# Ranks computed beside the counts, independent stores, and record scatters moved later, in a sigmoid-attention and top-1 MoE kernel

## The chip, the cores and the metric

The kernel runs on one core of one Trainium2 chip. The metric is the device time of one execution in microseconds (us). Three runs of the kernel before took 776.0, 776.97 and 777.6 us; their median, 776.97 us, is the time before. Engines are named as the profile names them: PE (TensorE matmul), PEld (its weight load), DVE (VectorE), ACT (ScalarE), POOL (GpSimd) and SP (SyncE, which here only issues DMAs).

## The reference

```python
# q, k, v: (8 batches, 12 heads, 448 tokens, 64); w_gate (768, 8); w1 (8, 768, 1024); w2 (8, 1024, 768)
scores = scale * np.matmul(q, k.transpose(0, 1, 3, 2)) - np.log(S)
attn = 1.0 / (1.0 + np.exp(-scores))
x = matmul(attn, v).transpose(0, 2, 1, 3).reshape(3584, 768)
logits = x @ w_gate
expert_idx = np.argmax(logits, axis=1)
gate_w = softmax(logits)[expert_idx]            # one weight per token
for e in range(8):                              # every token goes through its own expert only
    mask = expert_idx == e
    out[mask] = gate_w[mask, None] * (np.maximum(x[mask] @ w1[e], 0.0) @ w2[e])
```

## The kernel before, in words

**Two streams on PE.** Attention is cut into 168 steps. A step is one chunk of 64 keys for two pairs of heads: `scores(s)` (L616) and `weighted(s)` (L632), each with matmuls on 64x64 quarters of the array, which show as 8 records in each of the two lines. Seven steps finish two pairs of heads, 21 steps (`PB`) a batch. Steps 0 to 69 run attention alone, in the order written in `attention()`; from step 70 (`START`) each step also yields 14 matmuls of the dense part (`MIX`), and the seven attention chunks of two pairs come in one burst, once in seven steps. The dense part, `moe(b, wts)` (L240 and L263), takes seven batches of tokens through the expert that most of their tokens chose, with 448-column matmuls in three float32r terms. Its w1 loop runs over 8 columns j of 18 matmuls, and its weights come as raw tiles over SP, are split into a high part by ACT (L159) and a low part by POOL or DVE (L160), three w1 columns ahead. Whatever token did not choose that expert goes through two items of 256 rows at the end (`large`), found through a list of records.

**The gate of a batch** is a chain of small stages that `PLACES` puts at fixed steps: `gate_a` (logits, psg, L291), `gate_b` (transposed logits pl, L300, and the one-hot choice `oh`), `gate_c` (a matmul of `ones` by `oh`, L335, gives the counts; their maximum gives the expert), `gate_c2` (the mask `ce` and `lm = oh * ce`, the tokens that need a record), `gate_c3` (the gate weights), `gate_d` (two control matmuls of `upper` and of `ones` by `lm`, L388 and L389, then the ranks from PSUM, L392 to L403, giving the slot indices `si`), `gate_d2` s0 to s3 (POOL's indirect scatter of the records, L424, after an iota on POOL and a copy of the gates by DVE, L416), and `gate_g`, `gate_e` (the gate rows). The psg, pl, pc and pr tiles are taken by `small_ps` out of the four PSUM buffers `sc` of the scores. `upper` and `ones` are full 128-wide operands, so these matmuls use the whole array and stand between the quarter-array ones of attention or the dense ones.

**Queues.** All instructions stand in the order written (`manual_schedule`). SP issues weights, q, k, v, the token stores `x_tok<-xt` (L499, four DMAs for every three pairs of heads, 64 in all), the slot loads `raw<-x_tok` (L465) and the output stores (L218, 84). POOL issues some of the k and v loads before step 70, the records, and the low parts. `apart` declares that a store need not wait for earlier ones in a list: one list for each of the 12 column blocks (`stored`), and `taken[i]` one for each quarter of the token rows.

**Records before.** `PUTS` puts batch 0's four scatters at steps 34 to 40 and batch 1's at steps 56 to 62 (their places 13, 15, 17, 19 made even), while attention runs alone; those of batches 2 to 7 stand in the dense part. The tiles `si` and `rec` have two buffers each.

Of the kernel before, what the change touches and what calls it, by code (L numbers as in the profile page):

```python
# [18 lines left out]
P = 128  # L19
# [5 lines left out]
def tile_sigmoid_attention_top1_moe(  # L25
# [182 lines left out]
                self.split += 1  # L208

    stores = []  # L210
    stored = {}
    out_b = out.rearrange("(b j r) f -> b r j f", b=B, r=32)

    def store():
        if stores:
            n, d, i, ob = stores.pop(0)
            cols = slice(d * DW + i * DW // 4, d * DW + (i + 1) * DW // 4)
            put = nc.sync.dma_start(  # L218
                out_b[bass.ds(maps[n], 1)][:, :, :, cols].rearrange("o r j f -> (o r) j f"),
                ob.rearrange("p j s t -> p j (s t)")[32 * i : 32 * (i + 1)],  # L220
            )
            apart(put, stored.setdefault((d, i), []))

    def moe(b, wts):

# [101 lines left out]
    def gate_c(b, oh, z):  # L327
        def tl(nm, shape, dt=F32):
            return small.tile(shape, dt, tag=nm, name=f"{nm}_{b}")

        s1, s2 = tl("s1", [GP, NCH, E]), tl("s2", [GP, NCH, E])
        nc.scalar.activation(s1, z, AF.Sigmoid)
        nc.scalar.activation(s2, z, AF.Sigmoid, scale=-1.0)
        pc = small_ps(b, "pc")
        nc.tensor.matmul(pc[:, : NCH * E], ones[:GP], oh.rearrange("p c e -> p (c e)"), start=True, stop=True)  # L335
        cnt = tl("cnt", [P, E])
        nc.vector.tensor_reduce(cnt, pc[:, : NCH * E].rearrange("p (c e) -> p e c", e=E), axis=AX.X, op=ALU.add)
        cm = tl("cm", [P, 1])
        nc.vector.tensor_reduce(cm, cnt, axis=AX.X, op=ALU.max)
        ce = tl("ce", [P, E])  # L340
        nc.vector.scalar_tensor_tensor(ce, cnt, cm, rev, op0=ALU.is_equal, op1=ALU.mult)
        cr, was, now = top[:, b : b + 1], free[:, b : b + 1], free[:, b + 1 : b + 2]
        nc.vector.tensor_reduce(cr, ce, axis=AX.X, op=ALU.max)
        ri = tl("ri", [P, 2], I32)
        if b > 0:
            rf = tl("rf", [P, 2])
            old = top[:, b - 1 : b]
            nc.vector.tensor_sub(rf[:, 0:1], old, cr)
            nc.vector.scalar_tensor_tensor(rf[:, 0:1], rf[:, 0:1], was, cr, op0=ALU.mult, op1=ALU.add)
            nc.vector.tensor_scalar(ri[:, 0:1], rf[:, 0:1], -1.0, float(E), op0=ALU.mult, op1=ALU.add)  # L350
            nc.vector.tensor_scalar(ri[:, 1:2], was, -1.0, float(b), op0=ALU.mult, op1=ALU.add)
        return s1, s2, ri, ce, cm

    def gate_c2(b, oh, s1, s2, ri, ce, cm):
        def tl(nm, shape, dt=F32):
            return small.tile(shape, dt, tag=nm, name=f"{nm}_{b}")

        cr, was, now = top[:, b : b + 1], free[:, b : b + 1], free[:, b + 1 : b + 2]
        nc.vector.tensor_scalar(ce, ce, cr, None, op0=ALU.is_equal)
        keep = tl("keep", [P, 1])  # L360
        if b < B - 1:
            nc.vector.scalar_tensor_tensor(keep, cm, float(2 * P), was, op0=ALU.is_le, op1=ALU.mult)
        else:
            nc.vector.tensor_copy(keep, was)
        nc.vector.tensor_sub(now, was, keep)
        nc.vector.tensor_scalar(keep, keep, -1.0, None, op0=ALU.add)
        nc.vector.tensor_scalar(ce, ce, keep, 1.0, op0=ALU.mult, op1=ALU.add)
        lm = tl("lm", [GP, NCH, E], BF16)
        nc.vector.tensor_tensor(lm, oh, ce[:GP].unsqueeze(1).broadcast_to([GP, NCH, E]), op=ALU.mult)
        return lm  # L370

    def gate_c3(b, s1, s2):
        nc.vector.reciprocal(s2, s2)
# [3 lines left out]
        nc.vector.tensor_scalar(sm, sm, 1e-9, None, op0=ALU.add)  # L377
        nc.vector.reciprocal(gates[:GP, b], sm)

    def gate_d(b, lm):  # L380

        def tl(nm, shape, dt=F32):
            return small.tile(shape, dt, tag=nm, name=f"{nm}_{b}")

        pr = small_ps(b, "pr")
        lmf = lm.rearrange("p c e -> p (c e)")
        nce = NCH * E
        nc.tensor.matmul(pr[:, :nce], upper[:GP], lmf, start=True, stop=True)  # L388
        nc.tensor.matmul(pr[:, nce : 2 * nce], ones[:GP], lmf, start=True, stop=True)  # L389
        pre = tl("pre", [P, NCH, E])  # L390
        tot = pr[:, nce : 2 * nce].rearrange("p (c e) -> p c e", e=E)
        nc.vector.tensor_copy(pre[:, 0], base)  # L392
        for c in range(1, NCH):
            nc.vector.tensor_add(pre[:, c], pre[:, c - 1], tot[:, c - 1])
        nc.vector.tensor_add(base, pre[:, NCH - 1], tot[:, NCH - 1])
        rk = tl("rk", [GP, NCH, E])
        nc.vector.tensor_add(rk, pre[:GP], pr[:GP, :nce].rearrange("p (c e) -> p c e", e=E))
        nc.vector.tensor_add(rk, rk, region[:GP])
        nc.vector.tensor_mul(rk, rk, lm)
        sl = tl("sl", [GP, NCH])  # L400
        nc.vector.tensor_reduce(sl, rk, axis=AX.X, op=ALU.add)
        si = small.tile([GP, NCH], U32, tag="si", bufs=2, name=f"si_{b}")
        nc.vector.tensor_scalar(si, sl, BIG, None, op0=ALU.add)  # L403
        return si
# [47 lines left out]
    xts = {}  # L452
    wholes = {}
    raws = {}
    taken = [[] for _ in range(4)]
    x_tok_b = x_tok.rearrange("(b j r) (i f) -> b i r j f", b=B, r=32, i=4)

    def load_slot(n, ri):
# [4 lines left out]
        for i in range(4):  # L463
# [1 line left out]
                raws[n][32 * i : 32 * (i + 1)].rearrange("r j t s -> r j (t s)"),  # L465
                x_tok_b[bass.ds(maps[n], 1), i].rearrange("o r j f -> (o r) j f"),
            )
            taken[i].append(got)

    low_parts = []  # L470

# [16 lines left out]
    def tokens(g, pv):  # L488
# [5 lines left out]
            xts[b] = xtpool.tile([P, NB, KH, 32], F32, tag="xt", bufs=2, name=f"xt_{b}_{n}")  # L494
        nc.vector.transpose(xts[b][:, :, t, :], pv[:, :S].rearrange("p (j s) -> p j s", s=32))  # L495
        if t == KH - 1:
            rows = x_tok[b * S : (b + 1) * S].rearrange("(j r) (i f) -> i r j f", r=32, i=4)
            for i in range(4):
                put = nc.sync.dma_start(  # L499
                    rows[i][:, :, n * KH * 32 : (n + 1) * KH * 32],  # L500
                    xts[b][32 * i : 32 * (i + 1)].rearrange("r j t s -> r j (t s)"),
                )
                for got in taken[i]:
                    tc.declare_no_dep(put.ins, got.ins, reason="the slots read earlier batches' tokens")

    def small_ps(b, name):

        return ps_sc.tile([P, 512], F32, tag="sc", name=f"{name}_{b}")
# [164 lines left out]
    def attention():  # L673
# [33 lines left out]
        def stage(what, b):  # L707
# [9 lines left out]
            elif what == "l" and b > 0:  # L717
                load_slot(b - 1, g["c"][2])
            elif what == "d":
                si_of[b] = gate_d(b, g["lm"])  # L720
            elif what[0] == "s":
                gate_d2(b, si_of[b], int(what[1]))
            elif what == "g" and b > 0:
# [3 lines left out]

        LATE = {8: "b", 10: "c", 11: ("l", "c2"), 12: "c3", 15: "d", 16: "g", 26: "e"}
        FOUR = ("s0", "s1", "s2", "s3")
        PUTS = 2 * (dict(zip((13, 15, 17, 19), FOUR)),) + 4 * (dict(zip((27, 28, 29, 30), FOUR)),)  # L730
        PUTS += (dict(zip((25, 26, 27, 28), FOUR)), {9: "s0", 10: "s1"})
        LAST = {3: "b", 5: "c", 6: ("l", "c2"), 7: "c3", 8: "d", 9: "g"}
        EARLY = {5: "b", 7: ("c", "c2"), 9: ("l", "c3"), 11: "d", 13: "g", 32: "e"}
# [26 lines left out]
        for s in range(N_ST + 11):  # L760
# [14 lines left out]
            elif s == START:  # L775
                weigh_to(a)
                score_to(a + 2)
                copy_tokens()
            yield s, MIX[0]
            if s >= START:  # L780
                b, r = divmod(s - 3 * PB, PB)
                b += 1
# [11 lines left out]
            if s in SPLITS:  # L794
                split_tokens(0, SPLITS.index(s), nc.vector.tensor_copy)
            yield s, MIX[1]
        order.close()

    wts = Weights([(lambda b=b: regs.get(b)) for b in range(B + 1)], NS)
# [382 lines left out]
```

## Time and profile before

| what | value |
|---|---|
| runs | 776.0, 776.97, 777.6 us (median 776.97) |
| the profiled execution's own time | 776.84 us |
| its span in the trace | 775.0 us |
| PE busy | 768.4 us (99%) |
| DVE, ACT, POOL busy | 373.9, 384.1, 349.6 us (48%, 50%, 45%) |
| granted TensorE clock | 1.00 (2.4 GHz) in nearly every stretch |
| DMA | 125.67 MB, mean 162 GB/s |

The span runs from the first to the last instruction. A matmul's busy time overlaps that of the next, so the distance from one start to the next is the measure of what an instruction costs PE, and the timeline shows these starts.

### The profile page before, as it was taken

How to read it: one execution, taken by the hardware profiler on the slowest of the kernel's cores; microseconds unless marked ns; L12 is line 12 of the kernel's file. 1: busy time of each engine (PE TensorE's matmuls, PEld its weight loads, DVE VectorE, ACT ScalarE, POOL GpSimd, SP SyncE). 2: the span in 40 equal slices, each digit the busy share in tenths (PEclk: the TensorE clock that was granted, in tenths of full speed). 3: DMA queues.
4: the chain of work that ended last, by engine and by line, in shares of the span. 5: the costliest groups of instructions: out<-in, count | busy, mean ns of one | idle time of the engine just before them, and what ended most of it. 6: DMA issues, size and time to landing. Idle time of an engine off the chain costs nothing. (4 is left out here: it accounts for less than half of the span.)

```text
span 775.0 us, 15532 instructions
## 1 busy us (share of the span) xinstructions
PE 768.4 (99%) x5586; PEld 593.3 (77%) x5586; DVE 373.9 (48%) x806; ACT 384.1 (50%) x688; POOL 349.6 (45%) x330
## 2 busy tenths in 40 slices
PE   9999999999999999999999999999999999999997
PEld 6555557687696786867868769677698999999996
DVE  2354584465264652537426384254736493244543
ACT  5877776645536455264443653545523342444451
POOL 8648554242352342531615316054265764664351
PEclk9999999999999999999999999999999999999999
DMA  9777798976758846587585876766167554655770
GB/s 207 169 160 157 171 251 197 210 171 154 169 129 173 201 107 166 139 190 168 116 194 84 193 169 144 183 168 166 38 171 170 157 146 118 202 143 155 220 223 38
DMA packets 311633, 125.67 MB, mean 162 GB/s; under 512 B 210062, under 2 KB 307006, under 8 KB 311552
## 3 DMA queue, kind: packets, MB, share of 16 engines
q1 hardware_dynamic: 305504, 112.42, 61.9%
q0 software_dynamic: 5760, 11.76, 5.4%
q8 instruction: 45, 0.74, 0.4%
q10 hardware_dynamic: 288, 0.46, 0.2%
q14 instruction: 36, 0.29, 0.1%
HBM read 102.49 MB, written 22.49 MB: 161 GB/s over the span
## 5 line engine op out<-in xcount | busy, mean ns | idle before, releaser
L602 ACT ACTIVATE at<-sc,bias_s 128x448 f32<-128x448 f32 x336 | 192.3, 633 | 107.4 <-PE sc L616 106.5
L160 POOL TENSOR_TENSOR w1l<-wst,w1h 128x768 fp32r<-128x768 f32 x72 | 132.7, 1853 | 173.9 <-ACT w1h L159 172.2
L160 POOL TENSOR_TENSOR w2l<-wst,w2h 128x512 fp32r<-128x512 f32 x84 | 107.0, 1298 | 138.7 <-ACT w2h L159 121.0
L616 PE MATMUL sc<-qt,kt 64*64 64x448 f32 x1344 | 167.3, 545 | 0.0
L632 PE MATMUL av<-at,vn 64*64 64x448 f32 x1344 | 165.0, 536 | 0.0
L240 PE MATMUL ps<-xh,w1h 128*128 128x448 f32 x336 | 124.4, 370 | 0.2 <-DVE nw L439 0.2
L240 PE MATMUL ps<-xh,w1l 128*128 128x448 f32 x336 | 123.4, 367 | 0.0
L240 PE MATMUL ps<-xl,w1h 128*128 128x448 f32 x336 | 123.3, 367 | 0.0
L263 PE MATMUL ps<-hh,w2l 128*128 128x448 f32 x336 | 123.3, 367 | 0.0
L263 PE MATMUL ps<-hl,w2h 128*128 128x448 f32 x336 | 123.2, 367 | 0.0
L263 PE MATMUL ps<-hh,w2h 128*128 128x448 f32 x336 | 122.7, 365 | 0.0
L616 PEld LDWEIGHTS sc<-qt,kt 64*64 64x64 f32 x1344 | 78.2, 189 | 56.9 <-issue 44.4
L632 PEld LDWEIGHTS av<-at,vn 64*64 64x64 f32 x1344 | 59.4, 133 | 64.3 <-issue 53.5
L159 ACT CAST w2h<-wst 128x512 fp32r<-128x512 f32 x108 | 64.7, 620 | 75.7 <-PE ps L263 64.5
L247 ACT ACTIVATE hh<-ps 128x448 fp32r<-128x448 f32 x56 | 30.6, 546 | 139.6 <-PE ps L240 137.0
L276 DVE TENSOR_TENSOR ps<-ps,gt 128x448 f32<-128x448 f32 x42 | 40.7, 969 | 85.4 <-PE ps L263 85.3
L495 DVE STREAM_TRANSPOSE xt<-av 128x448 f32<-128x448 f32 x46 | 27.3, 629 | 101.5 <-PE av L632 100.4
L248 DVE SCALAR_TENSOR_TENSOR hl<-ps,hh 128x448 fp32r<-128x448 f32 x56 | 34.4, 614 | 78.3 <-ACT hh L247 76.8
L240 PEld LDWEIGHTS ps<-xh,w1h 128*128 128x128 f32 x336 | 63.1, 188 | 9.9 <-issue 4.4
L263 PEld LDWEIGHTS ps<-hh,w2l 128*128 128x128 f32 x336 | 65.2, 194 | 6.6 <-issue 3.5
L263 PEld LDWEIGHTS ps<-hl,w2h 128*128 128x128 f32 x336 | 65.2, 194 | 6.2 <-issue 3.2
L263 PEld LDWEIGHTS ps<-hh,w2h 128*128 128x128 f32 x336 | 65.2, 194 | 3.4 <-DVE nw L439 0.2
(158 smaller groups left out, 918.9 us busy)
## 6 DMA issues: line engine op xcount, KB each, us to landing
wst<-in_moe_w_dram SPq DMA_DIRECT2D x72, 384.0 KB, 3.3
wst<-in_moe_w_dram SPq DMA_DIRECT2D x54, 512.0 KB, 5.1
x_tok<-xt SPq DMA_DIRECT2D x64, 168.0 KB, 2.8
qn<-in_q_dram SPq DMA_DIRECT2D x184, 56.0 KB, 3.1
raw<-x_tok SPq DMA_DIRECT2D x28, 336.0 KB, 6.2
out_dram<-ob SPq DMA_DIRECT2D x84, 112.0 KB, 2.4
kn<-in_k_dram SPq DMA_DIRECT2D x104, 56.0 KB, 3.3
kn<-in_k_dram POOLq DMA_DIRECT2D x80, 56.0 KB, 4.0
```

Of the source, the lines that this page charges most:

```text
L159: nc.scalar.copy(hi, st)
L160: eng.tensor_tensor(lo, st, hi.bitcast(F32), op=ALU.subtract)
L240: nc.tensor.matmul(ps[:, :S], a[:, ws], b_, start=(t == 0 and n == 0), stop=(t == KD - 1 and n == 2))
L247: nc.scalar.activation(hh[:, :S], ps[:, :S], AF.Relu)
L248: nc.vector.scalar_tensor_tensor(hl[:, :S], ps[:, :S], 0.0, hh[:, :S].bitcast(F32), op0=ALU.max, op1=ALU.subtract)
L263: nc.tensor.matmul(ps[:, :S], a, b_, start=(j == 0 and n == 0), stop=(j == KF - 1 and n == 2))
L276: nc.vector.tensor_tensor(by_gate, by_gate, gate_rows[b], op=ALU.mult)
L495: nc.vector.transpose(xts[b][:, :, t, :], pv[:, :S].rearrange("p (j s) -> p j s", s=32))
L602: nc.scalar.activation(at, ps[:, :S], AF.Sigmoid, bias=bias_s, scale=SCALE)
L616: nc.tensor.matmul(ps[quarter(g, h), :S], ks, ops[g, "q"][OWN[h]], start=True, stop=True)
L632: nc.tensor.matmul(psv[g][OWN[h], :S], ops[g, "v"][rows, c, :], at[rows], start=(c == 0), stop=(c == KC - 1))
```

## The change

The matmul of `upper` moves from `gate_d` into `gate_c`, beside that of `ones`, and works on `oh` in place of `lm`; both results are copied into an SBUF tile `sums`. `gate_d` has no matmul left and reads `sums`. The running base of the lists grows by the masked counts `cnt * ce`, which `gate_c2` forms. `lm` becomes float32. All output stores are declared independent of each other, and all token stores of all slot loads; each output store and each group of four token stores has an SP nop in front. Token stores are issued by `keep_tokens`, after the next yield of `attention`, in place of directly behind the last transpose. Batch 0's scatters go to steps 70, 72, 74, 76 and batch 1's to 80, 82, 84, 86.

```diff
-    stored = {}
+    stored = []
...
     def store():
...
+            nc.sync.nop()
             put = nc.sync.dma_start(
...
-            apart(put, stored.setdefault((d, i), []))
+            apart(put, stored)
...
         pc = small_ps(b, "pc")
-        nc.tensor.matmul(pc[:, : NCH * E], ones[:GP], oh.rearrange("p c e -> p (c e)"), start=True, stop=True)
+        nce = NCH * E
+        for n, of in enumerate((ones, upper)):
+            nc.tensor.matmul(
+                pc[:, n * nce : (n + 1) * nce], of[:GP], oh.rearrange("p c e -> p (c e)"), start=True, stop=True
+            )
+        sums = tl("sums", [P, 2, NCH, E])
+        nc.vector.tensor_copy(sums.rearrange("p n c e -> p (n c e)"), pc[:, : 2 * nce])
         cnt = tl("cnt", [P, E])
-        nc.vector.tensor_reduce(cnt, pc[:, : NCH * E].rearrange("p (c e) -> p e c", e=E), axis=AX.X, op=ALU.add)
+        nc.vector.tensor_reduce(cnt, sums[:, 0].rearrange("p c e -> p e c"), axis=AX.X, op=ALU.add)
...
-        lm = tl("lm", [GP, NCH, E], BF16)
+        lm = tl("lm", [GP, NCH, E])
         nc.vector.tensor_tensor(lm, oh, ce[:GP].unsqueeze(1).broadcast_to([GP, NCH, E]), op=ALU.mult)
+        nc.vector.tensor_mul(cnt, cnt, ce)
...
-    def gate_d(b, lm):
+    def gate_d(b, lm, sums, cnt):
...
-        pr = small_ps(b, "pr")
-        lmf = lm.rearrange("p c e -> p (c e)")
-        nce = NCH * E
-        nc.tensor.matmul(pr[:, :nce], upper[:GP], lmf, start=True, stop=True)
-        nc.tensor.matmul(pr[:, nce : 2 * nce], ones[:GP], lmf, start=True, stop=True)
         pre = tl("pre", [P, NCH, E])
-        tot = pr[:, nce : 2 * nce].rearrange("p (c e) -> p c e", e=E)
         nc.vector.tensor_copy(pre[:, 0], base)
         for c in range(1, NCH):
-            nc.vector.tensor_add(pre[:, c], pre[:, c - 1], tot[:, c - 1])
-        nc.vector.tensor_add(base, pre[:, NCH - 1], tot[:, NCH - 1])
+            nc.vector.tensor_add(pre[:, c], pre[:, c - 1], sums[:, 0, c - 1])
+        nc.vector.tensor_add(base, base, cnt)
         rk = tl("rk", [GP, NCH, E])
-        nc.vector.tensor_add(rk, pre[:GP], pr[:GP, :nce].rearrange("p (c e) -> p c e", e=E))
+        nc.vector.tensor_add(rk, pre[:GP], sums[:GP, 1])
...
-    taken = [[] for _ in range(4)]
+    taken = []
...
         if t == KH - 1:
+            to_keep.append((b, n, xts[b]))
+
+    def keep_tokens():
+        while to_keep:
+            b, n, xt = to_keep.pop(0)
             rows = x_tok[b * S : (b + 1) * S].rearrange("(j r) (i f) -> i r j f", r=32, i=4)
+            nc.sync.nop()
             for i in range(4):
                 put = nc.sync.dma_start(...)
-                for got in taken[i]:
+                for got in taken:
...
-        PUTS = 2 * (dict(zip((13, 15, 17, 19), FOUR)),) + 4 * (dict(zip((27, 28, 29, 30), FOUR)),)
+        PUTS = tuple(dict(zip(range(r, r + 8, 2), FOUR)) for r in (START - PB, START + 10 - 2 * PB)) + 4 * (dict(zip((27, 28, 29, 30), FOUR)),)
...
             yield s, MIX[0]
+            keep_tokens()
             if s >= START:
...
             yield s, MIX[1]
+        keep_tokens()
```

## Rows read from the trace of the kernel before

**Rows 1.** The page's first part: busy us, share of the span, instructions.

```profile
PE 768.4 (99%) x5586; PEld 593.3 (77%) x5586; DVE 373.9 (48%) x806; ACT 384.1 (50%) x688; POOL 349.6 (45%) x330
```

**Rows 2.** Waits of PE, whole span: total us, times, longest us.

```profile
PE ps_warm L593 <- DVE ones L76: 1.1, 1, 1.1
PE ps L240 <- DVE nw L439: 0.2, 1, 0.2
```

**Rows 3.** Stretches of 25 us: length, busy us and instructions by engine, clock, DMA.

```profile
100.00:125.00 25.00, 25.00 (x276) 13.40 (x270) 16.58 (x32) 19.70 (x37) 17.05 (x21) 1.00 1.05 231
```

**Rows 4.** Waits of SP's queue, whole span.

```profile
SPq L218 <- DMA out_dram<-ob: 82.2, 50, 5.9
...
SPq L499 <- DMA raw<-x_tok: 36.4, 5, 8.1
```

**Rows 5.** Waits of all engines, whole span: POOL's for the record copy.

```profile
POOL recs L424 <- DVE rec L416: 43.8, 4, 18.3
```

**Rows 6.** Two stretches of equal length, attention alone, columns as in rows 3.

```profile
54.94:63.20 8.26, 8.26 (x86) 4.27 (x82) 6.49 (x25) 6.78 (x14) 4.55 (x9) 1.00 0.56 117
63.20:71.46 8.26, 8.26 (x93) 4.81 (x88) 3.40 (x6) 6.67 (x14) 7.65 (x12) 1.00 0.49 123
```

**Rows 7.** PE in order of time, batch 0's count: start us, us, instruction.

```profile
51.58 1.70 PE L632 MATMUL av<-at,vn 64*64 64x448 f32 x16
53.22 0.19 PE L335 MATMUL pc<-oh,ones 112*128 112x32 bf16 x1
53.34 1.79 PE L616 MATMUL sc<-qt,kt 64*64 64x448 f32 x16
54.95 0.93 PE L632 MATMUL av<-at,vn 64*64 64x448 f32 x8
```

**Rows 8.** PE in order of time, batch 1's ranks.

```profile
94.98 1.82 PE L632 MATMUL av<-at,vn 64*64 64x448 f32 x14
96.73 0.19 PE L388 MATMUL pr<-lm,upper 112*128 112x32 bf16 x1
...
96.88 2.13 PE L616 MATMUL sc<-qt,kt 64*64 64x448 f32 x16
98.49 0.92 PE L632 MATMUL av<-at,vn 64*64 64x448 f32 x6
```

**Rows 9.** PE in order of time, batch 2's ranks, in the dense part.

```profile
161.37 0.37 PE L240 MATMUL ps<-xl,w1h 128*128 128x448 f32 x1
161.58 0.19 PE L388 MATMUL pr<-lm,upper 112*128 112x32 bf16 x1
161.62 0.18 PE L389 MATMUL pr<-lm,ones 112*128 112x32 bf16 x1
161.64 0.45 PE L240 MATMUL ps<-xh,w1l 128*128 128x448 f32 x1
161.93 0.36 PE L240 MATMUL ps<-xh,w1h 128*128 128x448 f32 x1
```

**Rows 10.** Groups by line and shape: a DVE copy out of PSUM.

```profile
L312 DVE COPY lg<-pl 112x32 f32<-112x32 f32 x8 | 1.5, 184 | 9.1 <-PE pl L300 9.1
```

**Rows 11.** Tile pr: its readers' durations in ns, min/median/max.

```profile
L394 DVE TENSOR_TENSOR pre<-pre,pr x24: 161/161/165, 60.2 to 592.6; 128x8 f32<-128x8 f32 x24
```

**Rows 12.** Line 399, a product of two SBUF tiles, in the same form.

```profile
L399 DVE TENSOR_TENSOR rk<-rk,lm x8: 191/191/1203, 61.4 to 593.3; 112x32 f32<-112x32 f32 x8
```

**Rows 13.** Line 424, the record scatters: from issue to landing.

```profile
DMA to landing us min/median/max: 2.6/3.2/7.5
```

**Rows 14.** DVE in order of time at step 70, with the idle time before.

```profile
124.07 1.18 DVE L495 STREAM_TRANSPOSE xt<-av 128x448 f32<-128x448 f32 x2 [5.99 <-PE av L632]
```

**Rows 15.** POOL in order of time, the fourth low part of w1.

```profile
131.09 1.84 POOL L160 TENSOR_TENSOR w1l<-wst,w1h 128x768 fp32r<-128x768 f32 x1 [5.13 <-ACT w1h L159]
```

**Rows 16.** DVE in order of time, the last batch's ranks.

```profile
593.75 1.47 DVE L403 TENSOR_SCALAR si<-sl 112x4 uint32<-112x4 f32 x1
```

**Rows 17.** PE in order of time, just behind them.

```profile
595.80 0.47 PE L240 MATMUL ps<-xh,w1h 128*128 128x448 f32 x1 [0.19 <-DVE nw L439]
```

More of the change, by code (lines that the diff above doesn't have):

```diff
@@ L351, in gate_c, with gate_c2 @@
             nc.vector.tensor_scalar(ri[:, 1:2], was, -1.0, float(b), op0=ALU.mult, op1=ALU.add)
-        return s1, s2, ri, ce, cm
-    def gate_c2(b, oh, s1, s2, ri, ce, cm):
+        return s1, s2, ri, ce, cm, sums, cnt
+    def gate_c2(b, oh, s1, s2, ri, ce, cm, sums, cnt):
         def tl(nm, shape, dt=F32):
@@ L367, in gate_c2 @@
         nc.vector.tensor_scalar(ce, ce, keep, 1.0, op0=ALU.mult, op1=ALU.add)
-        lm = tl("lm", [GP, NCH, E], BF16)
+        lm = tl("lm", [GP, NCH, E])
         nc.vector.tensor_tensor(lm, oh, ce[:GP].unsqueeze(1).broadcast_to([GP, NCH, E]), op=ALU.mult)
-        return lm
+        nc.vector.tensor_mul(cnt, cnt, ce)
+        return lm, sums, cnt
     def gate_c3(b, s1, s2):
@@ L467, in load_slot @@
             )
-            taken[i].append(got)
+            taken.append(got)
     low_parts = []
@@ L496, in tokens @@
         if t == KH - 1:
+            to_keep.append((b, n, xts[b]))
+    to_keep = []
+    def keep_tokens():
+        while to_keep:
+            b, n, xt = to_keep.pop(0)
             rows = x_tok[b * S : (b + 1) * S].rearrange("(j r) (i f) -> i r j f", r=32, i=4)
+            nc.sync.nop()
             for i in range(4):
@@ L500, in tokens @@
                     rows[i][:, :, n * KH * 32 : (n + 1) * KH * 32],
-                    xts[b][32 * i : 32 * (i + 1)].rearrange("r j t s -> r j (t s)"),
+                    xt[32 * i : 32 * (i + 1)].rearrange("r j t s -> r j (t s)"),
                 )
-                for got in taken[i]:
+                for got in taken:
                     tc.declare_no_dep(put.ins, got.ins, reason="the slots read earlier batches' tokens")
@@ L719, in stage @@
             elif what == "d":
-                si_of[b] = gate_d(b, g["lm"])
+                si_of[b] = gate_d(b, *g["lm"])
             elif what[0] == "s":
```

## Prediction

> **What bounds the kernel now.** I read the page's busy shares first: PE is busy 768.4 of 775.0 us and DVE, ACT and POOL half of it at most [rows 1]. A pipelined PE can look busy while it waits, so the waits of PE come next: over the whole span they are 1.1 us at the start and 0.2 us once [rows 2]. The stretches of 25 us say the same where DMA is fullest: from 100 to 125 us PE has 25.00 of 25.00 us, at full clock, with ACT at 19.70 and DVE at 16.58 [rows 3]. Third, the starts in PE's timeline: attention alone runs at a steady pitch, 88 weight loads, one for each matmul, in 8.26 us, or 0.0939 us for each [rows 6]; dense matmuls follow each other at about 0.21 us [rows 9]. So the end is set by how many matmuls PE has to start and by what breaks that pitch. Only what takes an instruction out of PE's stream, or lets PE wait less, can shorten the run; SP's waits, however long [rows 4], are not waits of PE.
>
> The sum is made against the profiled execution's own 776.84 us, 1.84 us above its span. The median of the runs shown is 776.97 us, 0.13 us more.
>
> **The two matmuls taken out of gate_d.** What they cost differs between the two parts of the run.
>
> Dense part, batches 2 to 7. From the first of the pair to the second dense matmul behind it 0.35 us pass (161.58 to 161.93), where one dense matmul before them has 0.21 (161.37 to 161.58) [rows 9]. The pair costs 0.14 us; six batches give 0.84 us.
>
> Attention alone, batch 0. Two stretches of 8.26 us, one with the pair and one without, hold 80 attention matmuls (82 loads less the pair's two) and 88 [rows 6]. Eight are missing: 8 x 0.0939 = 0.75 us. Batch 1: from 94.98 to 98.49 us are 3.51 us with 14 + 16 attention matmuls, worth 2.82 us; the pair costs 0.69 us [rows 8].
>
> Why so much: a control matmul uses the whole array, so all four quarters must end before it and start again after it. One alone, where the quarters run in step, costs 3.37 us (51.58 to 54.95) less 32 x 0.0939 = 3.00, so 0.37 us [rows 7]. With 0.03 for the second that makes 0.40. The rest, 0.35 us in batch 0 and 0.29 in batch 1, I take for quarters that had come out of step and are brought together at the pair. I count it as saved too, since the next full-array matmuls in attention alone, the 24 of psg, stand behind an interruption of the pattern of their own; if it is only paid later, it comes back (second rival).
>
> Removed in all: 0.84 + 0.75 + 0.69 = 2.28 us.
>
> **The matmul added in gate_c.** The second of a pair adds between 0.02 us (161.62 to 161.64) and 0.04 us (161.58 to 161.62) [rows 9]; I take 0.03, and eight batches give 0.24 us. The net is 2.28 - 0.24 = 2.04 us.
>
> **DVE's work.** Added in each batch: the copy into `sums`, 64 columns out of PSUM where a copy of 32 takes 0.184 us [rows 10], so between 0.18 and twice that; and the product `cnt * ce`, between the 0.161 us of an addition as small [rows 11] and the 1.203 us of the longest product of SBUF tiles [rows 12]. I take 0.2 + 0.16 = 0.36 us, near the medians. Behind both stand the low parts `hl` of the dense part, which free PE's accumulators, and the slot's registers. I cost them at nothing: DVE, at 16.58 of 25 us, has the room [rows 3], and PE's only wait of this kind is the one of 0.2 us [rows 2]. That one is at the last batch: the indices `si` take 1.47 us instead of 0.17 or so and the next `hl` comes late [rows 16, 17]. There DVE works through c3 and d in one go, and uncovered the added time would go onto PE. In gate_d itself the count of DVE's additions stays, and its wait for PE goes, so I leave that 0.2 us as it is. `lm` in float32 I take at nothing: a product with it has the shape and the other operand it had, 0.191 us at the median and 1.203 at most [rows 12].
>
> At the additions of gate_d a rule speaks against the change. The 24 additions that read a PSUM tile took 161 to 165 ns, all of them [rows 11]; the product of two SBUF tiles a few instructions on, in the same chain, went up to 1203 ns, and `si` to 1.47 us [rows 12, 16]. The Trainium skill, in "SBUF — State Buffer", section "Who interferes with whom", says that a DVE instruction with two SBUF inputs contends with a GpSimd instruction that reads SBUF, and that the later one is held until the other is done. The trace agrees with it by the 1203 ns. By that rule five additions of each batch, now safe, can be held as the product is. Without holds the sum stays at 2.04 us; what a hold would do is the third rival, from rows alone.
>
> **Stores.** 84 output stores no longer wait for earlier ones, and 64 token stores no longer for slot loads: 82.2 and 36.4 us of waiting go from SP's queue [rows 4]. Weights, q, k and v behind them issue earlier. PE waits for none of these loads [rows 2], so this gains nothing, and I take 0; by the same cover the 84 + 16 nops cost nothing. The trace before has no nop; a hundred of them lie between 0 and the 118.6 us of SP time that goes [rows 4], nearer to 0. Should SP become late, what is next is a raw weight tile, then ACT's and POOL's parts, then PE.
>
> **Token stores a step later.** Before step 70 a group is issued in the same step, behind the two score steps. In the dense part it is issued behind the next 14 dense matmuls, 14 x 0.21 = 2.9 us, and past whatever weight loads and stores SP gets there; it no longer holds those up while it waits for DVE's transposes. The slot load that reads the rows stands some 13 steps behind, over 38 us. 0 us either way; the last batch's slot load, at place 6, still has eight.
>
> **Record scatters moved.** Eight scatters, two iotas and two small copies leave attention alone, where POOL also issues k and v. PE does not wait for these loads, so this gains nothing. They come to steps 70 to 86. For batch 0, DVE had been idle for 5.99 us before the transposes at 124.07 us, so the record's copy goes right behind them, at about 125.3 us [rows 14]; and POOL was idle for 5.13 us before the low part at 131.09 us [rows 15], which holds the first scatter. A new wait arises: batch 2's `si` (step 78) takes the buffer of batch 0's, whose last scatter is now at step 76. Two steps are 5.8 us; a scatter lands 3.2 us after its issue, 7.5 at most [rows 13]. So 0 us at the median and up to 1.7 us of DVE's time, with `hl` behind it, at worst. I take 0.
>
> **Sum.** 776.84 - 2.04 = 774.80 us, or 774.8; the span should become about 773.0.
>
> **Rivals.**
> *Out-of-step quarters are only paid later.* For it: they would still meet psg. Against: psg pays for its own interruption already. The early gain is then 2 x 0.40, the total 0.80 + 0.84 - 0.24 = 1.40: 775.4 us.
> *ACT paces attention alone,* and nothing is gained there. For it: 19.70 of 25 us [rows 3]. Against: it is not 25, and the pitch in attention alone is steady. Left is 0.84 - 6 x 0.03 = 0.66: 776.2 us.
> *An addition of the last batch's gate_d is held by POOL,* and DVE's chain stands still for one more low part, 1.84 us [rows 15]. For it: in that chain `si` is already held and PE behind it already late [rows 16, 17]. Against: one low part at most, in one batch. 774.80 + 1.84 = 776.6 us.
> *Slower: POOL is stuck at batch 0's first scatter at step 70,* waiting for DVE's copy, with the low part of w1's fourth column behind it. POOL did wait up to 18.3 us for such a copy [rows 5]. Of these, 5.13 are idle now [rows 15]; the low part has two columns of 18 matmuls, 36 x 0.21 = 7.6 us, from its call to its use, of which it needs 1.84. PE would wait 18.3 - 5.1 - 5.8 = 7.4 us: 782.2 us. It decides from a hold of 10.9 us on. Against: DVE is free there [rows 14].
> *Better:* the later flush at psg shrinks as well (0.29 to 0.35 us) and the last batch's wait goes (0.2): about 774.2 us.
>
> **How the numbers follow.** Forecast 0.55, paid later 0.15, ACT 0.09, held addition 0.06, POOL or another queue late 0.06, better 0.09. A difference of 0.2%, 1.55 us, is about what a measurement of this kernel can tell from none: the bound is 775.4 us. Faster is the forecast, the better case and a few of the paid-later ones, less the forecast's own spread: 0.63. Same is most of paid later, ACT and the held addition: 0.30. Slower 0.07. The range, 773.7 to 776.3, takes in everything but most of the held addition, the slow case and the outer spread of the runs.
>
> **What would show it.** After: no control matmul between gate_c and the next batch, and two of them side by side in gate_c; some 0.7 us less from 54 to 64 us and again from 94 to 99 us, PE's start of the dense part 1.4 us earlier; 0.14 us less at each later gate_d; SP's waits at L218 gone with nothing moving on PE for it. Wrong if PE shows a new wait for DVE or POOL, above all at 125 to 170 us or at the last batch, or if psg takes over what gate_d gave back.

## The result: slower by 0.75%, and what the profile after shows

Six runs of the changed kernel took 781.53 to 784.2 us, median 782.66; six of the kernel before have 776.98. The ratio is 1.0075 [1.0062, 1.0088]. The forecast was 774.8 us with a range from 773.7 to 776.3: the change was to make the kernel faster and makes it slower. The profiled execution took 782.35 us, its span is 780.5.

PE is as full as before, beside [rows 1]:

```profile
PE 769.4 (99%) x5578; PEld 597.7 (77%) x5578; DVE 391.4 (50%) x822; ACT 384.7 (49%) x688; POOL 349.0 (45%) x330
```

Eight matmuls are gone, as they should be. What is new stands in the waits of PE over the whole span (total us, times, longest), where the kernel before had two [rows 2]:

```profile
PE ps L264 <- DVE nw L441: 1.7, 1, 1.7
PE sc L627 <- DVE logits L296: 1.7, 1, 1.7
PE ps_warm L604 <- DVE ones L76: 1.1, 1, 1.1
PE ps L241 <- DVE nw L441: 0.6, 1, 0.6
PE turn_k L592 <- DMA kn<-in_k_dram: 0.2, 1, 0.2
PE psg L292 <- ACT xf L665: 0.2, 1, 0.2
```

Two waits of 1.7 us for DVE are new, the wait of 0.2 us at the last batch has become 0.6, and two short ones for a load of k and for ACT have come in; the wait for `ones` was there before. To place them I subtract the start of every dense matmul in the profile before from that of the same matmul after; below this is "the lag", above zero where the kernel is later than before. PE's first `av` already starts between 0.87 us earlier and 0.33 us later in the traces of this document than in the one before, ahead of any gate, so a lag of that size need not come of an edit; how a lag changes inside one trace is free of this. The lag is +1.47 us at the first dense matmul (125.79 us before), +5.05 behind batch 2's ranks (169.44), +5.18 at 496.79 and +5.29 at 595.80, of a span 5.5 us longer. So nearly all is lost in two places.

**From 104 to 127 us.** Up to batch 2's psg the change gained: psg starts at 113.91 instead of 115.71 us. Its last eight matmuls wait for ACT's `xf`, so that the scores behind it start only 0.87 us ahead (116.11 for 116.98). Then DVE, in order of time:

```profile
104.54 0.65 DVE L479 STREAM_TRANSPOSE whole<-raw 128x448 f32<-128x448 f32 x1 [2.14 <-DMA raw<-x_tok]
...
116.50 2.15 DVE L483 TENSOR_TENSOR xl<-whole,xh 128x448 fp32r<-128x448 f32 x1
118.58 0.63 DVE L581 STREAM_TRANSPOSE kt<-kn 128x448 f32<-128x448 f32 x1
119.14 0.35 DVE L296 COPY logits<-psg 128x224 f32<-128x224 f32 x1
```

and POOL and PE at the same time:

```profile
116.37 1.81 POOL L160 TENSOR_TENSOR w1l<-wst,w1h 128x768 fp32r<-128x768 f32 x1 [5.08 <-ACT w1h L159]
```

```profile
119.54 0.65 PE L627 MATMUL sc<-qt,kt 64*64 64x448 f32 x2 [1.65 <-DVE logits L296]
```

DVE waits 2.14 us for the rows of batch 0, which it did not before, so its last `xl` starts 0.13 us behind POOL's first low part and takes 2.15 us. Before, the `xl` came first:

```profile
116.08 0.63 DVE L481 TENSOR_TENSOR xl<-whole,xh 128x448 fp32r<-128x448 f32 x1
```

The copy of the logits stands behind it on DVE, and PE's next scores need the buffer which that copy frees.

**From 161 to 175 us, batch 2's ranks.** DVE and POOL of the changed kernel:

```profile
162.35 3.50 DVE L396 TENSOR_TENSOR pre<-pre,sums 128x8 f32<-128x8 f32 x3
165.77 0.16 DVE L397 TENSOR_TENSOR base<-base,cnt 128x8 f32<-128x8 f32 x1
165.89 0.19 DVE L399 TENSOR_TENSOR rk<-pre,sums 112x32 f32<-112x32 f32 x1
166.12 1.17 DVE L400 TENSOR_TENSOR rk<-rk,region 112x32 f32<-112x32 f32 x1
167.32 1.21 DVE L401 TENSOR_TENSOR rk<-rk,lm 112x32 f32<-112x32 f32 x1
...
169.54 0.58 DVE L249 SCALAR_TENSOR_TENSOR hl<-ps,hh 128x448 fp32r<-128x448 f32 x1
```

```profile
161.91 0.95 POOL L426 DMA_INDIRECT recs<-rec,si  x1 [0.15 <-issue]
162.88 2.54 POOL L160 TENSOR_TENSOR w2l<-wst,w2h 128x512 fp32r<-128x512 f32 x2
165.89 2.59 POOL L160 TENSOR_TENSOR w2l<-wst,w2h 128x512 fp32r<-128x512 f32 x2 [0.47 <-ACT w2h L159]
```

Three additions that took 161 to 165 ns each out of PSUM [rows 11] take 3.50 us together; the addition of `region` (L400) and the product with `lm` (L401) are held as well. Nearly all of the 3.50 us is one instruction, as the durations of the three in ns show (min/median/max):

```profile
L396 DVE TENSOR_TENSOR pre<-pre,sums x3: 168/168/3098, 162.4 to 165.7; 128x8 f32<-128x8 f32 x3
```

It starts at 162.35 us, while the scatter runs on POOL, and ends at 165.45, with the second of the two low parts behind the scatter (165.42). The product with `lm` ends at 168.53 us, POOL's last low part at 168.48, and `hl` starts at 169.54 us. In the kernel before:

```profile
161.83 0.56 DVE L394 TENSOR_TENSOR pre<-pre,pr 128x8 f32<-128x8 f32 x3 [1.05 <-PE pr L389]
164.47 0.58 DVE L248 SCALAR_TENSOR_TENSOR hl<-ps,hh 128x448 fp32r<-128x448 f32 x1
```

PE of the changed kernel stands still, and then runs slowly:

```profile
168.07 0.37 PE L241 MATMUL ps<-xh,w1l 128*128 128x448 f32 x1
170.18 0.48 PE L264 MATMUL ps<-hh,w2h 128*128 128x448 f32 x1 [1.74 <-DVE nw L441]
...
172.26 0.57 PE L264 MATMUL ps<-hl,w2h 128*128 128x448 f32 x1
172.63 0.57 PE L264 MATMUL ps<-hh,w2l 128*128 128x448 f32 x1
```

The stretches there (columns as in rows 3) give the clock:

```profile
168.00:171.00 3.00, 1.26 (x7) 0.85 (x6) 2.84 (x9) 0.55 (x1) 0.56 (x2) 1.00 0.63 109
171.00:174.50 3.50, 3.50 (x12) 3.08 (x11) 3.40 (x8) 0.00 (x0) 0.96 (x1) 0.51 1.13 319
```

For 3.4 us the granted clock is at its lower level (1.2 GHz), and matmuls follow each other at 0.37 us. The lag goes from 1.47 to 3.39 at the wait and on to 5.05 in the slow stretch.

**What moved on the queues.** The waits at the output stores (L218, [rows 4]) are gone; other waits of SP have grown, above all this one, which was 45.3 us:

```profile
SPq L183 <- POOL w2l L160: 102.6, 21, 13.2
```

And one difference that I had no term for shows in the stretch from 20 to 35 us, in the kernel before and after (columns as in rows 3; the last two are the DMA engines' share and GB/s):

```profile
20.00:35.00 15.00, 15.00 (x164) 8.16 (x162) 6.27 (x11) 12.90 (x25) 9.40 (x16) 1.00 0.63 138
```

```profile
20.00:35.00 15.00, 15.00 (x161) 8.74 (x157) 7.19 (x12) 12.95 (x24) 11.45 (x19) 1.00 1.31 161
```

The DMA engines are busy twice as long (0.63 to 1.31) for 17% more bytes, with attention alone and no scatter or output store in sight; the loads of k that POOL issues there land 5.1 us after their issue instead of 2.6 (medians). `sums` (256 bytes a partition) and the wider `lm` (64) had pushed the tiles allotted behind them, `kn`, `qn`, `vn` and `xt`, up by 320 bytes: the pool of `kn` and `qn` starts at byte 178752 of a partition instead of 178432, which is 64 instead of 0 modulo 128, and `kn` and `qn` arrive in pieces of 128 bytes.

### The profile page after: what moved, and what is told of

Same layout as the page of the kernel before. It is cut to its first block, busy times and chain, and to the rows that moved or that the text cites. A ratio compares the mean times of both kernels' runs of the same rounds, so it can differ in the third digit from the quotient of the medians.

```text
span 780.5 us, 15522 instructions
## 1 busy us (share of the span) xinstructions
PE 769.4 (99%) x5578; PEld 597.7 (77%) x5578; DVE 391.4 (50%) x822; ACT 384.7 (49%) x688; POOL 349.0 (45%) x330
## 5 line engine op out<-in xcount | busy, mean ns | idle before, releaser
L627 PE MATMUL sc<-qt,kt 64*64 64x448 f32 x1344 | 171.2, 544 | 1.7 <-DVE logits L296 1.7
L643 PE MATMUL av<-at,vn 64*64 64x448 f32 x1344 | 168.4, 537 | 0.0
L627 PEld LDWEIGHTS sc<-qt,kt 64*64 64x64 f32 x1344 | 80.7, 189 | 59.5 <-issue 45.4
L643 PEld LDWEIGHTS av<-at,vn 64*64 64x64 f32 x1344 | 62.0, 133 | 60.5 <-issue 49.3
```

Source lines behind the costliest of these rows:

```text
L627: nc.tensor.matmul(ps[quarter(g, h), :S], ks, ops[g, "q"][OWN[h]], start=True, stop=True)
L643: nc.tensor.matmul(psv[g][OWN[h], :S], ops[g, "v"][rows, c, :], at[rows], start=(c == 0), stop=(c == KC - 1))
```

## The experiments

Theories from the profile after: (H) DVE instructions reading two SBUF tiles are held by POOL; (E) the moved scatters let `xl` meet POOL's first low part; (A) the shifted addresses. The lags, in us, are of the one profiled execution of each, at dense matmuls named by their start in the trace before.

| kernel | median us | ratio to before | lag at 125.79 | at 169.44 | at 496.79 | at 595.80 |
|---|---|---|---|---|---|---|
| changed | 782.66 | 1.0075 [1.0062, 1.0088] | +1.47 | +5.05 | +5.18 | +5.29 |
| stores_only | 776.89 | 0.9997 [0.9988, 1.0006] | -0.30 | -0.30 | -0.28 | -0.43 |
| ranks_only | 781.97 | 1.0050 [1.0037, 1.0063] | +1.78 | +1.79 | +4.99 | +5.11 |
| scat_only | 781.15 | 1.0053 [1.0038, 1.0068] | +1.57 | +1.60 | +1.86 | +1.71 |
| no_ranks | 779.42 | 1.0025 [1.0011, 1.0038] | +1.78 | +1.80 | +1.80 | +1.80 |
| pad_only | 780.11 | 1.0035 [1.0022, 1.0048] | +0.97 | +0.70 | +3.30 | +3.17 |
| aligned | 780.44 | 1.0040 [1.0027, 1.0052] | +1.60 | +3.50 | +3.31 | +3.41 |
| reduces | 780.55 | 1.0043 [1.0030, 1.0056] | +1.89 | +2.96 | +3.13 | +2.92 |
| mended | 779.32 | 1.0030 [1.0020, 1.0040] | +2.01 | +3.15 | +2.54 | +2.18 |
| no_race | 777.82 | 1.0008 [0.9999, 1.0016] | +0.67 | +0.67 | +0.69 | +0.54 |
| ranks_aligned | 777.74 | 1.0003 [0.9994, 1.0012] | -1.16 | -1.27 | +0.45 | +0.71 |
| ranks_outs | 776.18 | 0.9985 [0.9975, 0.9995] | -0.82 | -0.98 | -1.08 | -0.99 |
| aligned_back | 776.55 | 0.9985 [0.9976, 0.9993] | +1.96 | +1.79 | +1.61 | +1.70 |
| best | 776.70 | 0.9990 [0.9980, 0.9999] | -0.45 | -0.60 | -0.78 | -0.68 |

**One part at a time.** stores_only is the kernel before with the nops, the independent stores and the later token stores; ranks_only and scat_only are it with the new gate_c, gate_c2 and gate_d, or with the new PUTS; no_ranks is the changed kernel with the three gates as before:

```diff
-        PUTS = 2 * (dict(zip((13, 15, 17, 19), FOUR)),) + ...          # scat_only: this line alone
+        PUTS = tuple(dict(zip(range(r, r + 8, 2), FOUR)) for r in (START - PB, START + 10 - 2 * PB)) + ...
```

> The kernel before with the change's stores alone: independent output stores, token stores a step later, nops; gate and scatters as before. Theories A, H and E: SP's waits at the stores go, PE does not wait for what SP loads: 776.5 to 777.5 us, the same as before, DMA share 0.6 to 0.7 from 20 to 35 us. Rival Q (weights that come sooner let ACT and POOL split sooner, and POOL's parts meet DVE's chains elsewhere): 778 us and more, with PE waiting for DVE somewhere.

> The kernel before with the ranks beside the counts alone; stores, token stores and scatters as before. Theory H: batch 2's gate_d is held as in the changed kernel if POOL's low parts of w2 run beside it, which they do in the kernel before too (one addition there took 0.53 us): the three additions take 1.5 to 3.5 us, PE waits 0 to 1.7 us: 775 to 779 us. Theory S: without moved scatters nothing is late, and what the two matmuls cost comes back: 774.8 us, faster than before by 2 us. Theory Q: no loss before 127 us.

> The kernel before with batch 0's and batch 1's record scatters at steps 70 to 86, nothing else changed. Theory H: no addition reads two SBUF tiles, so no wait of PE at batch 2's gate_d: 776 to 778 us, the same as before within 0.2%. Theory S: POOL's low parts come later by one or two scatters of 0.95 us and PE waits in 155 to 175 us as in the changed kernel: 779 to 783 us.

> The changed kernel with gate_c, gate_c2 and gate_d as before (two control matmuls of lm in gate_d, additions out of PSUM); stores, token stores and the places of the scatters as changed. Theory H (held additions): the 3.6 us that PE loses at batch 2's gate_d (a wait of 1.7 us and 3.4 us at half the clock) go, while the two pairs in attention alone cost their 1.4 us again and the loss around 114 to 127 us may stay (1.5 to 3.3 us): 778 to 780 us, with pre<-pre,pr at 161 to 165 ns. Theory S (the moved scatters put POOL's low parts in another phase and late): PE still waits for DVE or POOL between 155 and 175 us: 782 to 784 us. Theory Q (queues: unblocked stores and token stores make q, k, v and raw tiles late): a loss of 1.5 to 3.3 us before 127 us stays here and not in ranks_only.

The stores alone do nothing. Ranks and scatters each lose about 0.5% alone; with the change's stores beside them the scatters lose 0.25% (no_ranks), and no run shows why. In scat_only the loss of the trace is there by 125.79 us: `xl` starts at 116.60, 0.14 us behind POOL's low part, takes 2.15 us, and PE waits 1.6 us for the logits; no_ranks has the same (E). The profiled execution of scat_only (778.79 us) is the fastest of its six, so the trace shows less than half of the 4.1 us between the medians. In ranks_only, 781.97 us where the theories gave 774.8 to 779, the scatters are at their old places, and `xl` is held all the same, here on DVE and POOL:

```profile
116.81 2.15 DVE L482 TENSOR_TENSOR xl<-whole,xh 128x448 fp32r<-128x448 f32 x1
116.68 1.80 POOL L160 TENSOR_TENSOR w1l<-wst,w1h 128x768 fp32r<-128x768 f32 x1 [3.27 <-ACT w1h L159]
```

PE waits 1.10 us for the logits there, and 0.80 us for a load of v (`vn`) ahead of it. So the moved scatters are one way into this meeting and not the only one. At batch 2's ranks scat_only has POOL at the same work as the changed kernel, but its additions read PSUM:

```profile
161.84 0.94 POOL L424 DMA_INDIRECT recs<-rec,si  x1 [0.15 <-issue]
162.80 2.55 POOL L160 TENSOR_TENSOR w2l<-wst,w2h 128x512 fp32r<-128x512 f32 x2
```

```profile
163.18 0.56 DVE L394 TENSOR_TENSOR pre<-pre,pr 128x8 f32<-128x8 f32 x3 [1.01 <-PE pr L389]
163.78 0.16 DVE L395 TENSOR_TENSOR base<-pre,pr 128x8 f32<-128x8 f32 x1
163.85 0.18 DVE L397 TENSOR_TENSOR rk<-pre,pr 112x32 f32<-112x32 f32 x1
164.07 1.34 DVE L398 TENSOR_TENSOR rk<-rk,region 112x32 f32<-112x32 f32 x1
```

They take 0.56 us, not 3.50, beside the same low parts; the next instruction with two SBUF tiles, the addition of `region`, is held. The Trainium skill, "SBUF — State Buffer", section "Who interferes with whom", has it so: a DVE instruction with two SBUF inputs contends with a GpSimd instruction that reads SBUF. The trace agrees, with 0.56 us against 3.50. ranks_only and ranks_aligned have the new additions without the moved scatters and lose nothing there (lag +1.78 to +1.79, and -1.16 to -1.27): in ranks_aligned the additions are held for 2.60 us, two of them by one low part each, but the low parts, with no scatter ahead of them, are over earlier, and `hl` starts at 164.76 with no wait of PE. So batch 2's loss needs both parts of the change.

**Additions with one SBUF input.** The changed kernel, with each running sum as a reduction over `base` and the counts in one tile (32 bytes larger, so that the tiles behind lie at 96 modulo 128):

```diff
-            nc.vector.tensor_add(pre[:, c], pre[:, c - 1], sums[:, 0, c - 1])
+            nc.vector.tensor_reduce(pre[:, c], sums[:, : c + 1].rearrange("p c e -> p e c"), axis=AX.X, op=ALU.add)
```

> The changed kernel with one thing changed: the running base stands as a first row in front of the totals in the tile sums, and each of the three additions of gate_d is a tensor_reduce over the first rows, an instruction with one SBUF input (a copy of base is added in gate_c). Theory H: the three take 0.16 to 0.2 us each, at most one or two later products are held, PE's wait at batch 2's gate_d and the half clock behind it go: 778.5 to 780 us, 3 to 4 us less than the changed kernel. Theory S and theory Q: no difference to the changed kernel, 781.5 to 784 us.

The three reductions are not held, though the scatter runs beside them (162.12 to 163.07 us); the next addition of two SBUF tiles is:

```profile
162.37 0.37 DVE L398 TENSOR_REDUCE pre<-sums 128x8 f32<-128x16 f32 x3
162.65 3.03 DVE L401 TENSOR_TENSOR base<-base,cnt 128x8 f32<-128x8 f32 x1
```

The hold passes on to the next instruction that takes two tiles, and is shorter in sum: PE waits 1.2 us instead of 1.7, with no slow stretch, and the lag grows by 1.07 instead of 3.58 us. H holds, though the mend is half of one: 2.1 us off the changed kernel's median, where 3 to 4 were expected.

**Addresses.** pad_only is the kernel before with an unused tile of 320 bytes ahead of the pools; aligned the changed kernel, and ranks_aligned ranks_only, with one of 192 bytes (320 + 192 = 512, again 0 modulo 128).

```diff
+    small.tile([P, 80], F32, tag="pad", name="pad")      # 48 in aligned and ranks_aligned
     ident = const.tile([P, P], F32, name="ident")
```

> The kernel before with one unused tile of 320 bytes a partition in the pool small, as much as sums and the wider lm take, so that q, k, v and the token tiles lie 320 bytes higher (64 bytes off the 128-byte rows in which q and k arrive) and nothing else differs. Theory A (addresses): the ranks slow the DMAs by where their tile pushes the others. Then from 20 to 35 us the DMA share is 1.25 to 1.35 here as in ranks_only (1.30), not 0.63 as before, the slots' raw rows land late, the last low part xl of the first batch meets POOL's first low part and PE waits about 1.7 us for the logits: 778.5 to 781 us. Rival (the instructions of the ranks, or chance of the run): share 0.6 to 0.7 and 777 us.

> The changed kernel with an unused tile of 192 bytes in small, so that the tiles behind lie 512 bytes higher than before and all as they lay to each multiple of 128 bytes. Theory A: the DMA share from 20 to 35 us falls from 1.31 to 0.6 to 0.7. The moved scatters still bring the early race (as in scat_only, 1.6 us at 116 us) and the held additions the wait at batch 2: 780 to 782 us, 1 to 2 us less than the changed kernel and steadier. Rival: no difference, 781.5 to 784 us, share 1.3.

> The kernel before with the ranks beside the counts and an unused tile of 192 bytes in small, which brings the addresses behind back to multiples of 128 bytes; stores and scatters as before. Theory (addresses, and holds only where the moved scatters push POOL's low parts into batch 2's gate_d): DMA share 0.6 to 0.7 from 20 to 35 us, no wait of PE at batch 2, no late q, k or v; what gate_d gives back is left: 774.8 to 776.5 us, 4 us or more under ranks_only. Rival (two-input additions are held wherever they stand): PE waits 1 us or more at a gate_d, 778 us and more.

The stretch of 20 to 35 us, in pad_only and then in ranks_aligned:

```profile
20.00:35.00 15.00, 15.00 (x162) 7.58 (x157) 7.16 (x12) 12.91 (x24) 11.11 (x19) 1.00 1.28 162
```

```profile
20.00:35.00 15.00, 15.00 (x164) 8.24 (x160) 6.28 (x11) 12.88 (x25) 9.67 (x17) 1.00 0.64 141
```

An unused tile alone doubles the DMA share and costs 0.35%; 192 bytes more give share and time back: ranks_only falls from 1.0050 to 1.0003, the changed kernel from 1.0075 to 1.0040. So A is one cause and not the only one. pad_only's time came as expected and its path did not: `xl`, which was to meet POOL's low part, is not held (0.63 us, ahead of it). Its trace loses 0.68 us between 33 and 45 us and again at 308, 0.95 before batch 2's psg, and 1.49 at batch 7's logits (below). In aligned PE waits 2.0 us at batch 2 and no slow stretch follows; why the same wait is followed by the lower clock in one and not in the other stays open. The slow stretch is 1.66 us of the changed kernel's lag, and at 169.44 the lags of the two differ by 1.55; so this pair is weaker evidence for the price of the addresses than ranks_only with ranks_aligned, or pad_only.

**Scatters and the first low parts.** mended joins reduces, a tile of 160 bytes and the first of three low parts a step later; no_race is scat_only with the first two later:

```diff
-    FIRST = (START - 5, START - 3, START - 1)
+    FIRST = (START - 3, START - 2, START - 1)      # mended: START - 4, START - 3, START - 1
```

> The changed kernel with all three suspected costs taken away: the unused tile (160 bytes here) that brings the addresses back, the additions as reductions of one SBUF input, and the first w1 column split at step 66 instead of 65, so that POOL's first low part does not run beside the last xl of the first batch. Theories A, H and E (the early race) together: PE waits neither at 116 us nor at batch 2's gate_d, what gate_d gave back remains: 774.5 to 776.5 us, the best of all. If one more cost of the change is unknown, 778 us and more, with PE's wait to show where.

> scat_only (the kernel before with the scatters moved) with the first three w1 columns split at steps 67, 68 and 69 instead of 65, 67 and 69, so that POOL's first low part comes behind the last xl of batch 0 in ACT's order. Theory: the early loss of 1.6 us is this meeting of the two: xl takes 0.63 us instead of 2.15, PE does not wait for the logits, and the run is at 776.5 to 778 us against scat_only's 781.15. Rival (the loss comes from DMAs in another order, raw rows late): PE still starts the dense part 1.5 us late, 780 us and more.

mended, 779.32 us where 774.5 to 776.5 was expected, says nothing on E: its first low part did not move away, `xl` still took 2.16 us and PE waited 1.7. In no_race `xl` takes 0.63 us, no wait of PE for the logits is left, and 0.45% of scat_only's 0.53% goes. So the place of the first low parts is the cause in scat_only; that all of the 0.45% is this one wait no trace shows.

**Where the ranks' gain went.** With its addresses mended ranks_aligned is 1.16 us ahead at 125.79 us, and behind at 496.79; its median, 777.74 us, is above the 774.8 to 776.5 expected. DVE there, in the kernel before and in ranks_aligned:

```profile
486.14 0.65 DVE L277 STREAM_TRANSPOSE ob<-ps 128x448 f32<-128x448 f32 x1 [2.95 <-DMA out_dram<-ob]
486.72 0.35 DVE L295 COPY logits<-psg 128x224 f32<-128x224 f32 x1
```

```profile
487.03 0.65 DVE L278 STREAM_TRANSPOSE ob<-ps 128x448 f32<-128x448 f32 x1 [5.30 <-DMA out_dram<-ob]
487.61 0.35 DVE L296 COPY logits<-psg 128x224 f32<-128x224 f32 x1
```

The transpose waits for an older output store to land. Before, the copy of the logits came just in time; PE, now earlier, waits 0.9 us for it. ranks_outs makes only the output stores independent:

```diff
-    stored = {}
+    stored = []
...
+            nc.sync.nop()
             put = nc.sync.dma_start(
...
-            apart(put, stored.setdefault((d, i), []))
+            apart(put, stored)
```

> The kernel before with the ranks beside the counts, the 192-byte tile that keeps the tiles behind on their 128-byte places, and now also the output stores independent of each other (list and nop); scatters and token stores stay as before. What is open is where the time went that the ranks had gained by the start of the dense part (1.16 us ahead there, 0.45 us behind from 497 us on). Theory 'output stores': ahead of the copy of batch 7's logits DVE's transpose into ob waits for older output stores to land (5.30 us with the ranks, 2.95 in the kernel before, where the copy came just in time), and PE waits 0.9 us for the logits. With independent stores that wait falls to 1.5 us or less, PE's wait for the logits is gone, PE stays 1.0 to 1.5 us ahead of the kernel before at 497 us, the span is about 774.0 and the median 1.2 to 1.8 us under ranks_aligned: ratio to before 0.998 to 0.9995. Rival 'phase': the score buffers come round in another order at that place because PE arrives earlier, and the stores only look like the cause: DVE's wait falls, but PE still loses 1 us or more between 445 and 497 us, span 775.5, ratio 1.000.

```profile
483.00 0.65 DVE L279 STREAM_TRANSPOSE ob<-ps 128x448 f32<-128x448 f32 x1 [0.89 <-DMA out_dram<-ob]
485.10 0.39 DVE L297 COPY logits<-psg 128x224 f32<-128x224 f32 x1 [1.45 <-PE psg L293]
```

The wait falls to 0.89 us, DVE now waits for PE, the lead is kept (-1.08), and the kernel is 0.15% faster than before. The rival, PE's phase, falls. The same wait is 5.80 us in ranks_only and 4.86 in pad_only, which lose 2.4 and 1.5 us from 484.47 to 496.79, and 1.25 in the changed kernel, which loses none: its independent stores had mended what they alone seemed not to touch. In pad_only PE is 1.81 us late there, so an early PE is not the only thing that makes this wait longer.

**Without the moved scatters.** aligned_back is aligned with PUTS as before; best has the later FIRST as well.

> The kernel aligned (the changed kernel with its addresses brought back) with the record scatters of batches 0 and 1 at their old steps. Theory: batch 2's gate_d is held only together with the moved scatters, so the 2.1 us that PE lost there in aligned go, and with them the early wait for the logits, if POOL's loads go out as before: 774.5 to 776.5 us. Rival: the holds stay (2 us at batch 2) and only the early wait goes: 778 to 779 us.

> aligned_back with the first three w1 columns split at steps 67, 68 and 69: ranks beside the counts at the old addresses, the change's stores, the scatters where they were, and no meeting of xl with POOL's first low part. If all costs found are gone and the pairs' gain in attention alone is kept: 774.3 to 775.5 us, faster than before by 1.5 to 2.7 us. If the third part is late for the dense part, which begins right behind: 777 us and more, with PE waiting for POOL at 125 to 135 us.

Both beat the kernel before by a little; best, at 776.70 us, stays above its 774.3 to 775.5. aligned_back's profiled execution (779.02 us) is the longest of its eleven and met the hold of `xl`, so its lags don't stand for its median; best, without that meeting, has all its lags below zero. The intervals of ranks_outs, aligned_back and best overlap, so which of them is best is not told.

## Why the prediction was wrong, by its steps

**Right: the bound, and the matmuls' price.** PE's stream sets the end, and only waits and the pitch moved it. Attention alone should have given 1.44 - 0.06 = 1.38 us. Between 45 and 103 us the starts of the same `av` matmuls gain 1.55 to 1.58 us on the trace before in all nine kernels with the new ranks, and at most 0.01 in the five without. The rival "only paid later" falls with it, and so does "ACT paces attention alone"; psg's 24 matmuls take 1.34 us in before and in ranks_outs alike. What the forecast did not have is what becomes of the gain: ranks_aligned and ranks_outs start the dense part only 1.16 and 0.82 us ahead (the latter with a wait of 0.4 us for `vn`). In the dense part 0.66 was forecast; ranks_outs gains 0.61 up to the last batch's ranks (-0.82 to -1.43).

**Wrong: "I cost them at nothing: DVE, at 16.58 of 25 us, has the room".** A share of busy time says nothing of one chain. The chain of ranks has `hl` behind it and PE behind `hl`; the added 0.36 us (0.22 and 0.16 measured) is small beside some 5 us of holds at batch 2 (3.50 + 1.17 + 1.21 where the same five operations take 0.94 unheld). The prediction had the rule and made a rival of it, with a wrong place and price: the last batch, one low part, 1.84 us; only among its signs of being wrong did it name 125 to 170 us. There the additions take 0.57 us and it is the product with `lm` that is held:

```profile
598.24 1.85 DVE L401 TENSOR_TENSOR rk<-rk,lm 112x32 f32<-112x32 f32 x1
```

which makes PE's wait 0.63 instead of 0.19 us and gives back 0.44 of the ranks' gain. At batch 2 the chain ran into a scatter and four low parts on end, and cost 3.58 us with the stretch at the lower clock.

**Wrong: "PE does not wait for these loads, so this gains nothing", and 0 for the moved scatters.** I asked what the scatters waited for at their new place (the feared stand of POOL at step 70 did not come: POOL waits 43.7 us for `rec` in all, before 43.8) and not what POOL would do next to DVE without them, nor whom they push at step 76. At the old place `xl` started 0.86 us ahead of POOL's low part (116.08 and 116.94) and now starts 0.13 us behind it: a PE wait of 1.65 us, and in scat_only, by no_race, up to 0.45%. At the new place the scatter stands beside batch 2's ranks, with the low parts behind it. And that PE does not wait for the loads held only at PE's old pace. POOL issues a load of v behind the scatters, before and after:

```profile
112.50 0.61 POOL L558 DMA_DIRECT2D vn<-in_v_dram  x1
110.73 0.56 POOL L569 DMA_DIRECT2D vn<-in_v_dram  x1 [5.60 <-PE av L643]
```

Between 110 us and the start of batch 2's psg PE loses 0.4 to 2.0 us on the trace before in all seven experiments with the scatters at the old place (0.5 in ranks_aligned, 1.5 in ranks_outs), and nothing in the seven kernels that have them moved. So the move did give PE something; the changed kernel, 1.80 us ahead at psg, lost it to `xf` and the logits.

**Missing: a term for the new tile.** Nothing in the sum stood for where `sums` lies. It costs 0.35% in pad_only, and mending it gives 0.47% and 0.35% in the two pairs (1.0050 to 1.0003, 1.0075 to 1.0040), the last with the slow stretch in it.

**Half right: the stores at 0.** Alone they are (0.9997); with PE earlier the output stores are worth 0.18% or 1.4 us (1.0003 in ranks_aligned, 0.9985 in ranks_outs). SP's waits gave nothing; DVE's wait for the same stores, 2.95 us in the trace before, was cover that was just used up, and I did not look at it.

What stays open: why DVE waits for the rows of batch 0 after the change, 2.14 us (1.00 in scat_only, 1.21 in no_race, 1.47 in ranks_outs), and the clock after the wait at batch 2. DVE's first transpose of these rows starts between 104.49 and 105.06 us in the eight kernels whose `xl` is held, and no later than 104.12 in the others but no_race. No run has the moved scatters together with the additions out of PSUM, independent stores and the later first low parts.

## What to carry to other kernels

Ask of each chain that frees a buffer for the bounding engine what stands directly beside it on the other engines, not how busy its engine is: moving operands from PSUM to SBUF, or moving another engine's work by a few us, can turn 0.56 us into 3.50. Look for waits that end just in time in the profile before (a 2.95-us wait of DVE with none of PE behind it), since whatever makes the bounding engine earlier will meet them. And when a change adds a tile, compare the DMA share of a stretch that the change doesn't touch; if it moves, try an unused tile before any other theory.

## What the runs showed of the hardware that I had not expected

- Tiles filled in pieces of 128 bytes: with the tiles at 64 instead of 0 modulo 128 the DMA engines' share from 20 to 35 us goes from 0.63 to between 1.28 and 1.31 (pad_only, ranks_only, changed; 1.32 at 96 in reduces), and back to 0.60 to 0.64 at 0 modulo 128 (aligned, mended, ranks_aligned); all eleven kernels at 0 lie between 0.60 and 0.68. The Trainium skill, "DMA: Bandwidth & Descriptors", section "How a descriptor splits into AXI transactions", says that the first transaction of a descriptor which does not start on a 256-byte boundary starts at the boundary below and fetches bytes that are not used; that this is the cause no run here shows.
- A hold can last over more than one POOL operation: one addition of two SBUF tiles that starts while the scatter runs stands 3.10 us (3.19 in aligned, 3.03 in reduces), over the rest of the scatter and two low parts of 1.30 us. Where the additions start beside a low part, each is held by that one alone (1.15 and 1.22 us in ranks_aligned).
- An instruction with one SBUF operand can be held too: `si<-sl` took 1.47 us in the kernel before [rows 16] and 1.27 in scat_only, while reductions in the same chain were never held (0.16 to 0.20 us each in reduces).
- After a 1.74-us wait PE had 3.4 us at the lower clock in one kernel, and none after 2.0 us in another.
